# Four layers of memory attention and gated FFN on one core: beta as a row spread by a product, masks of two rounds merged, FFN norms in pairs of tiles, the order planned anew

## The chip, the cores and the metric

One core of one Trainium2 chip. The metric is the device time of one execution in microseconds (us). The time before is the median of three runs. A profile is of one execution; its span runs from the first to the last instruction that the profiler saw, and the execution's own time is a little longer.

## What is computed

`x` is 2048 x 512, bfloat16. Four blocks follow each other, attention, FFN, attention, FFN, each added to `x`, with the same weights both times:

```python
def _A_ref(x, wq, wk, wv, wo, beta):          # on layernorm(x)
    # 32 heads of 16; the sequence is 4 segments of L = 512
    phi = lambda t: jnp.where(t > 0, t + 1.0, jnp.exp(t))
    mask = (ar[:, None] < ar[None, :]) * -1e9
    g = sigmoid(beta)                          # one number for each head
    for s in range(4):
        p = softmax(qs @ ks.T * scale + mask)  # inside the segment
        a_dot = p @ vs
        a_mem = (phi(qs) @ M) / (phi(qs) @ z + 1e-6)
        o = g * a_mem + (1.0 - g) * a_dot
        M, z = M + phi(ks).T @ vs, z + phi(ks).sum()
    return concat(o) @ wo

def _B_ref(x, w_gate, w_up, w_down):           # on layernorm(x), F = 1792
    return (gelu(x @ w_gate) * (x @ w_up)) @ w_down
```

## The kernel before

**Steps.** A segment of 512 rows is four tiles of 128. Each of the 4 segments goes through two layers, so there are 8 attention steps `k` = 0 to 7 (`Att`) and 8 FFN steps (`Ffn`). Attention step k+4 needs FFN step k of the same segment, and step k needs the memory `M`, `z` of step k-1. Attention of later segments and the FFN of earlier ones run interleaved.

**An attention step.** The norm (`Norm`): statistics of the four tiles on VectorE, one small pair of instructions on GpSimd for all four (add eps, power -0.5, L526 and L531), then each tile is scaled (`xn`, L543) and transposed into `xnT`. That last step is either a DMA transpose issued from SP (L436), or four products with the identity on TensorE, `turn_item`, L585, whose result VectorE or ScalarE copies out (L460, L461); `BY_PE` and `pe_turns` say which. In `turn_item`, `FILL` = 2 products of 128 x 256 with the constant tile `warm` stand ahead of a tile's transposes for the steps in `BY_PE` (L583). Then products with w_q, w_k, w_v (L475 as one 128 x 128 product, L470 as four products of 32 columns side by side: function `product` takes the form that saves a change of tiling).

**Scores.** For each group `b` of 8 heads there are `ROUNDS` = 9 rounds of score products (L936): four for the even heads, one shared, four for the odd ones. They run two rounds at a time into four PSUM banks; ScalarE takes the exponential of both (L1394) into slots of `pt`. Rounds that touch the diagonal are masked there: `DIAG` gives 1, 1, 0 or 2 pieces of 64 columns to each of the four (GpSimd, L1341, one instruction for a round), and the shared round is masked whole, by VectorE with a triangle `tri` (L1351) or by GpSimd in two halves (L1346). A `flush` (L952) then multiplies the masked rounds with the values. The extra value columns, which hold `cden` = 1 + exp(beta), give the denominators.

**An FFN step.** w_o products and the addition to `x` (L1025), the norm as above, 14 tiles of w_gate products, whose results are copied to `gel_sb` and later go through gelu, a few of them straight from PSUM (`direct`), 14 tiles of w_up (multiplied in by VectorE, L1090), four tiles of w_down.

**The order.** All instructions are issued by a planner that runs when the kernel is built. `Clocks` and `Engine` keep an estimated time for each engine with a written-out cost for each instruction; `POLICY` holds weights, slacks and due times. TensorE's queue is filled item by item: scores when ScalarE's backlog is small, else the item that is most due and whose inputs are expected to be there, else, while scores remain, a filler product `warm` x `wide`, which computes nothing. The other engines' queues come from posted jobs, the most urgent first. Each queue runs strictly in the order that the planner wrote; waits are semaphores. A DMA transpose is expected to have landed 1.4 us plus `margin` after its issue:

```python
        def told(t2):
            t3 = max(t2 + 1.4 + margin, ck.dma + 1.2)
            ck.at(t3 - 0.2, lambda: landed(t3))
        ck.sp.post(t, slack, (1.45, lambda: nc.sync.dma_start_transpose(out=out(), in_=in_()), told))
```

**The front** is written by hand: the four tiles of segment 0 are loaded by SP and ScalarE's queue, and `beta` behind them from ScalarE's queue, copied to all 128 partitions (`beta_bc`). 15 fillers (L349) run on TensorE meanwhile. ScalarE computes the moments of one tile, then exp(beta) and exp(-beta) (L1200, L1201), then copies out the first two transposed tiles (L598); VectorE copies the other two (L600). The first products with w_k and w_q follow (L907, L912), and from there the planner takes over with starting times for each engine (`ck.pe = 10.45` and so on).

Of the kernel before, what the change touches and what calls it, by code (L numbers as in the profile page):

```python
# [12 lines left out]
ALU = mybir.AluOpType  # L13
# [29 lines left out]
DIAG = [1, 1, 0, 2]  # L43
SHARED = len(FULL)
# [20 lines left out]
FILL = 2  # L65
# [4 lines left out]
    flush_wait=22.067, piece_slack=7.095, kb_slack=20.572, mem_slack=-6.268, margin=2.476, qk_due=0.851,  # L70
    e_q=-1.002, e_k=1.306, exp_slack=-25.092, e_slack=4.951, phi_slack=10.885, gelu_slack=10.893,
    act_evict=5.208, first_evict=-3.627, gate_step=0.016, up_due=0.12, up_step=0.042, down_due=1.978,
    down_step=0.501, upd_due=1.364, kb_act=6.077, vz_slack=-6.198, x_dve=2.604, v0_due=-1.946, x1_at=-38.956,
    x2_at=16.871, x3_at=24.085, x3_load=17.807, direct=4, gelu_tiles=3, look=1.884, lag=0.5, wv_at=4.575,
    xn_pool=3.759, kb_pool=3.166, cut_pool=2.871, at_pool=10.151, pe_turns=2, gate_due=1.051, shun=1.318,
    hold=5, early=5.58, starve=0.305, near=-0.115, cap=2, soon=5.955, columns=1)
# [15 lines left out]
class Engine:  # L92
# [24 lines left out]
    def serve(self, now):  # L117

        self.jobs = [j for j in self.jobs if not j[4]]
        jobs = [j for j in self.jobs if not self.only or j[3] in (None, self.only)]  # L120
        if not jobs:
            return False
        start = max(self.free, min(j[0] for j in jobs) + self.LATENCY)
        if start > now:
            return False
        held = self.rival is not None and self.rival.port > start + 0.25
        job = min((j for j in jobs if j[0] + self.LATENCY <= start + 0.03), key=lambda j: j[0] + j[1] + (
            self.shun if held and isinstance(j[2][0][0], Port) else 0.0))
# [23 lines left out]
        return True  # L152


class Clocks:
# [36 lines left out]
    def serve(self):  # L192

        again = True
        while again:
# [4 lines left out]
            for w in list(self.waiting):  # L200
                if w[0]():
                    self.waiting.remove(w)
                    w[1]()
                    again = True
            first = min(self.engines, key=lambda e: max(e.free, min((j[0] for j in e.jobs), default=1e9)))
            again |= first.serve(self.pe) or any(e.serve(self.pe) for e in self.engines)
# [79 lines left out]
def order(pol, nc, cst, seg, wrk, psp, A_x, A_wq, A_wk, A_wv, A_wo, A_beta, B_x, B_w_gate, B_w_up, B_w_down, out):  # L286
# [15 lines left out]
    beta_bc = cst.tile([P, H], BF16, name="beta_bc")  # L302
# [12 lines left out]
    nc.scalar.dma_start(out=beta_bc[:], in_=A_beta.partition_broadcast(P))  # L315
# [35 lines left out]
    keep_warm(WARM, 0)  # L351

# [41 lines left out]
    def later_constants():  # L394
# [5 lines left out]
        for n, va in enumerate(vaugs[-1:] + vaugs[:-1]):  # L400
            ck.dve.post(12.0 + 3.0 * n, NORMAL, (0.4, lambda va=va: column(va), None))
# [98 lines left out]
    class Norm:  # L500
        def __init__(self, key, tt0, tag, slack, free):
            self.key, self.tt0, self.tag, self.slack, self.free = key, tt0, tag, slack, free
            self.mv, self.n, self.left = None, 0, TPS
# [4 lines left out]
        def stats(self, j, ready):  # L508
# [14 lines left out]
        def scales(self, ready):  # L523
            def first():
                self.ve = wrk.tile([P, TPS, 1], F32, tag="lnve", name="ve")
                nc.gpsimd.tensor_scalar(out=self.ve[:], in0=self.mv[:, :, 1:2], scalar1=EPS_LN, scalar2=None,  # L526
                                        op0=ALU.add)

            def second():
                self.rs = self.small("rs", 1)  # L530
                nc.gpsimd.tensor_tensor(out=self.rs[:], in0=self.ve[:], in1=mhalf[:], op=ALU.pow)  # L531

            ck.pool.post(ready, URGENT, (0.25, first, None),
                         (1.05, second, lambda t: ck.when(self.free, lambda: self.start(max(t, ck.pe)))))

        def start(self, ready):
            self.xnT = seg.tile([P, KT, L], BF16, tag=self.tag, bufs=1, name="xnT")
            for j in range(TPS):
# [35 lines left out]
        def turn_item(self, j, xn, t, landed):  # L574
# [7 lines left out]
            fill = FILL if self.key in BY_PE else 0  # L582
# [26 lines left out]
    class Att:  # L609
# [14 lines left out]
        def add_items(self):  # L624
# [54 lines left out]
            def v(j):  # L679
# [23 lines left out]
                def vz_sent(t):  # L703
                    self.n_vz += 1
                    t2 = max(t + 1.4 + pol.margin, ck.dma + 1.2)
                    if self.n_vz == 2:
# [3 lines left out]
                            lambda: ck.has(("xnTa", k, j)) and (k or ck.pe > max(pol.wv_at, 12.4)) and (k <= SETS or ("flush", k - SETS, 3, 1) in ev),  # L710
# [229 lines left out]
        def flush_item(self, b, par, places, masked):  # L940
# [4 lines left out]
            def mm():  # L945
                ck.tiling("columns")
                work = [(i + par * (SHARED + 1), self.vaug, *piece) for i, pieces in enumerate(FULL) for piece in pieces]
# [252 lines left out]
    nc.scalar.activation(out=tmp_e, in_=beta_bc[:], func=ACT.Exp)  # L1200
    nc.scalar.activation(out=tmp_e2[:], in_=beta_bc[:], func=ACT.Exp, scale=-1.0)  # L1201

# [18 lines left out]
    n0.first_turn(1)  # L1221
    n0.first_turn(2)
# [16 lines left out]
    ck.pe, ck.act.free, ck.dve.free, ck.pool.free, ck.sp.free = 10.45, 10.75, 10.5, 8.1, 7.6  # L1239
    banks[0:4] = [10.8, 9.45, 9.9, 10.4]  # L1240
    ev["q", 0, 0] = 10.35
    a0.n_qkv = 2
    a0.k_done(0, None, 10.75)
    later_constants()
    ck.dma = 13.0
# [18 lines left out]
    norm_of_input(1, max(pol.x1_at, 10.4), 0.5)  # L1264
    norm_of_input(2, max(pol.x2_at, 13.2), 1.0)
# [73 lines left out]
    def mask(slot, n):  # L1339
        view = pt_all[:, slot, :, 0:C * n].rearrange("p u (t c) -> p u t c", c=C)  # L1340
        nc.gpsimd.affine_select(out=view, in_=view, pattern=[[0, 4], [0, n], [1, C]], compare_op=ALU.is_ge,  # L1341
# [7 lines left out]
    def mask_both(slot):  # L1349
        view = pt_all[:, slot, :, :].rearrange("p u (t c) -> p (u t) c", c=C)  # L1350
        nc.vector.tensor_tensor(out=view, in0=view, in1=tri[:].unsqueeze(1).to_broadcast([P, 4 * TPS, C]), op=ALU.mult)  # L1351

    def post_mask(slot, t, at, done):
        n = round_of(t)[3]
        if n is None:
            taken = []
            ck.dve.post(at, pol.x_dve, (Port(0.67), lambda: mask_both(slot), done.append), taken=taken)
            ck.pool.post(at, NORMAL, (Port(1.14), lambda: mask_half(slot, 0), None), (Port(1.14), lambda: mask_half(slot, 1), done.append),
                         taken=taken)
        elif n:  # L1360
            ck.pool.post(at, NORMAL, (Port(0.245 + 0.215 * n), lambda: mask(slot, n), done.append))
        else:
            done.append(at)

    def score(n):
# [22 lines left out]
        for p, pair in enumerate(pairs):  # L1388
            score_banks.update(pair)
            for i in pair:  # L1390
                banks[i] = 1e9

            def exp(p=p, pair=pair):
                nc.scalar.activation(  # L1394
                    out=pt_all[:, s0:s0 + 2, 2 * p:2 * p + 2, :].rearrange("p r h c -> p h r c"),
# [127 lines left out]
```

## Time and profile before

| | |
|---|---|
| median of three runs | 549.18 us (548.96 to 549.21) |
| the profiled execution | 549.09 us, its span 547.4 us |
| TensorE products / weight loads | 533.9 / 277.9 us busy |
| VectorE, ScalarE, GpSimd | 444.8, 435.9, 307.4 us busy |
| DMA | 27.02 MB, 49 GB/s on average; 88 of the issues are transposes |

PE is TensorE, PEld its weight loads, DVE VectorE, ACT ScalarE, POOL GpSimd, SP the queue that issues most DMAs. A row of a group gives line, engine, operation, result and operands, shape, count, then busy time and mean length in ns of one, then the idle time of that engine before them with what ended it. Products are pipelined: one that is followed by another takes the time from its start to the next start, which is shorter than its own length.

### The profile page before, as it was taken

The page shows a single profiled execution, that of the slowest core. Times are in us where ns is not written, and L with a number is a line of the kernel's source. Part 1 is how long each engine was busy: PE and PEld are TensorE (multiplying, and loading weights), DVE is VectorE, ACT ScalarE, POOL GpSimd, SP SyncE. Part 2 cuts the span into 40 slices and gives each one's busy share as a digit, 9 for nine tenths or more (in the row PEclk, how much of TensorE's full clock was granted, in tenths as well). Part 3 has the DMA queues.
Part 4 walks back from the last instruction along what each step waited for, and adds up shares of the span by engine and source line. Part 5 has one row for each costly group of instructions (what it writes and reads, how often), then busy time and mean ns, then how long its engine had stood idle before and what let it go on. Part 6 is the DMA issues. An engine that isn't in the chain of part 4 may idle for free.

```text
span 547.4 us, 22326 instructions
## 1 busy us (share of the span) xinstructions
PE 533.9 (98%) x9794; PEld 277.9 (51%) x9852; DVE 444.8 (81%) x823; ACT 435.9 (80%) x545; POOL 307.4 (56%) x359
## 2 busy tenths in 40 slices
PE   8999999999999999999999999999999999999997
PEld 4454555454544455444544555544464455555544
DVE  6999898899999899759997887988888786686342
ACT  5899989988899987989899898897889984830330
POOL 2789489579843766528882487927874043400000
PEclk9999999999999999999999999999999999999999
DMA  8407600711231113501222241211311005100001
GB/s 254 111 2 178 151 12 3 175 42 23 50 50 22 23 32 51 79 2 25 41 31 40 32 61 23 31 38 36 70 48 28 2 10 89 26 4 21 20 0 40
DMA packets 64930, 27.02 MB, mean 49 GB/s; under 512 B 49216, under 2 KB 64832, under 8 KB 64832
## 3 DMA queue, kind: packets, MB, share of 16 engines
q1 hardware_dynamic: 64400, 25.31, 22.7%
q8 instruction: 77, 1.26, 1.0%
q10 hardware_dynamic: 432, 0.27, 0.2%
q14 instruction: 21, 0.17, 0.1%
HBM read 9.71 MB, written 2.10 MB: 22 GB/s over the span
## 4 chain that ended last, share of the span: by engine, by line
PE 85%; DVE 9%; issue 2%; DMA 2%; ACT 2%; POOL 0%; SPq 0%; DVEq 0%; POOLq 0%; ACTq 0%
PE ps L475 41%; PE ps L470 30%; PE ps L936 7%; PE ps L952 6%; DMA x_sb<-in_A_x_dram 2%; DVE st L513 2%; ACT pt L1394 1%; DVE x_sb L1025 1%; DVE byq L969 1%; DVE xn L543 1%; PE ps L585 1%; DVE phiq L743 1%; PE ps L583 1%; DVE vaug L460 0%; DVE kf L460 0%
## 5 line engine op out<-in xcount | busy, mean ns | idle before, releaser
L1394 ACT ACTIVATE pt<-ps 128x1024 bf16<-128x1024 f32 x288 | 279.7, 1028 | 41.0 <-PE ps L936 32.3
L1341 POOL TENSOR_SCALAR_AFFINE_SELECT pt<-pt 128x256 bf16<-128x256 bf16 (+1 forms) x192 | 111.9, 597 | 128.5 <-ACT pt L1394 126.8
L1090 DVE TENSOR_TENSOR gel_sb<-gel_sb,ps 128x512 bf16<-128x512 bf16 x112 | 74.5, 682 | 27.0 <-PE ps L475 21.3
L1346 POOL TENSOR_SCALAR_AFFINE_SELECT pt<-pt 64x1024 bf16<-64x1024 bf16 x50 | 60.9, 1218 | 11.8 <-ACT pt L1394 7.8
L475 PE MATMUL ps<-xnT,wg_sb 128*128 128x512 bf16 x266 | 63.6, 380 | 1.2 <-issue 0.8
L475 PE MATMUL ps<-xnT,wu_sb 128*128 128x512 bf16 x265 | 62.2, 380 | 1.5 <-issue 1.1
L1025 DVE TENSOR_TENSOR x_sb<-x_sb,ps 128x512 bf16<-128x512 bf16 (+1 forms) x68 | 43.0, 644 | 23.7 <-PE ps L475 16.7
L969 DVE STREAM_TRANSPOSE byq<-ps 128x512 f32<-128x512 f32 x64 | 45.3, 709 | 20.9 <-PE ps L952 18.9
L470 PE MATMUL ps<-wd_sb,gel_sb 128*32 128x512 bf16 (+1 forms) x1012 | 54.6, 356 | 0.0
L475 PE MATMUL ps<-wd_sb,gel_sb 128*128 128x512 bf16 (+1 forms) x240 | 49.8, 355 | 1.6 <-issue 1.6
L762 POOL TENSOR_SCALAR e<-e 128x512 bf16<-128x512 bf16 x29 | 46.0, 1587 | 1.1
L475 PEld LDWEIGHTS <-wu_sb 128*128 128x128 bf16 x278 | 25.9, 98 | 31.2 <-issue 1.1
L470 PE MATMUL ps<-xnT,wg_sb 128*32 128x512 bf16 x676 | 41.2, 380 | 0.0
L513 DVE BATCH_NORM_STATS2 st<-x_sb 128x6 f32<-128x512 bf16 x60 | 40.3, 672 | 1.0 <-DMA x_sb<-in_A_x_dram 0.9
L475 PEld LDWEIGHTS <-wg_sb 128*128 128x128 bf16 x279 | 25.8, 98 | 29.7 <-issue 0.6
L470 PE MATMUL ps<-xnT,wu_sb 128*32 128x512 bf16 x680 | 38.6, 379 | 0.0
L416 POOL TENSOR_SCALAR kx<-kf,masks 128x512 bf16<-128x512 bf16 x22 | 35.0, 1592 | 2.0 <-ACT kf L461 0.8
L952 PE MATMUL ps<-pt,vaug 128*32 128x256 bf16 (+2 forms) x1344 | 35.0, 238 | 0.0
L470 PEld LDWEIGHTS <-gel_sb 128*32 128x32 bf16 x1012 | 25.3, 97 | 17.7 <-issue 1.3
L475 PEld LDWEIGHTS <-gel_sb 128*128 128x128 bf16 x251 | 23.3, 98 | 21.6 <-issue 0.4
L1149 ACT ACTIVATE gel_sb<-gel_sb 128x1536 bf16<-128x1536 bf16 (+1 forms) x28 | 33.5, 1283 | 0.0
L543 DVE TENSOR_SCALAR xn<-x_sb,mv,rs 128x512 bf16<-128x512 bf16 x57 | 28.0, 538 | 6.3 <-POOL rs L531 4.0
(148 smaller groups left out, 899.0 us busy)
## 6 DMA issues: line engine op xcount, KB each, us to landing
vz<-vaug SPq DMA_DIRECT2D x14, 136.0 KB, 2.6
wg_sb<-in_B_w_gate_dram SPq DMA_DIRECT2D x8, 224.0 KB, 3.8
wu_sb<-in_B_w_up_dram SPq DMA_DIRECT2D x8, 224.0 KB, 3.8
wd_sb<-in_B_w_down_dram SPq DMA_DIRECT2D x7, 256.0 KB, 4.1
x_sb<-in_A_x_dram SPq DMA_DIRECT2D x3, 512.0 KB, 7.4
out_dram<-x_sb SPq DMA_DIRECT2D x12, 128.0 KB, 1.7
xnT<-xn SPq DMA_TRANSPOSE x40, 2.7
wk_sb<-in_A_wk_dram SPq DMA_DIRECT2D x2, 256.0 KB, 6.0
```

The costliest lines, as they stand in the source:

```text
L470: nc.tensor.matmul(out[r], lhsT=lhsT[:, r], rhs=rhs, start=start, stop=stop, tile_position=(0, 32 * c))
L475: nc.tensor.matmul(out, lhsT=lhsT, rhs=rhs, start=start, stop=stop)
L513: nc.vector.bn_stats(out=self.st6[:, 0, :], in_=x_sb[:, self.tt0 + j, :])
L762: lambda eng: eng.tensor_scalar(out=e[0][:], in0=e[0][:], scalar1=1.0, scalar2=None, op0=ALU.min), summed)
L936: nc.tensor.matmul(ps_all[:, bank, o + c0:o + c0 + n], lhsT=lhsT, rhs=self.q[rows, b, q0:q0 + n], start=True, stop=True, tile_position=(32 ...
L952: nc.tensor.matmul(ps()[32 * j:32 * j + 32, q0:q0 + n], lhsT=va[:, ki * VW + g:ki * VW + g + 32], rhs=pt_all[:, places[i], j, c0:c0 + n], ...
L969: nc.vector.transpose(out=self.byq[:, par, :, :].rearrange("p a c -> p (a c)"), in_=ps()[:])
L1025: ck.dve.post(ck.made(), slack, (0.15 + 0.00104 * (c1 - c0), lambda: nc.vector.tensor_tensor(out=xt, in0=xt, in1=ps()[:, 0:c1 - c0], op=AL ...
L1090: ck.dve.post(ck.made(), NORMAL, (0.683, lambda: nc.vector.tensor_tensor(out=g, in0=g, in1=ps()[:], op=ALU.mult), lambda t: (ps.read(t), e ...
L1341: nc.gpsimd.affine_select(out=view, in_=view, pattern=[[0, 4], [0, n], [1, C]], compare_op=ALU.is_ge, fill=0.0, base=C, channel_multiplier=-1)
L1346: nc.gpsimd.affine_select(out=view, in_=view, pattern=[[0, 4 * TPS], [1, C]], compare_op=ALU.is_ge, fill=0.0, base=0, channel_multiplier=-1)
L1394: nc.scalar.activation(out=pt_all[:, s0:s0 + 2, 2 * p:2 * p + 2, :].rearrange("p r h c -> p h r c"), in_=ps_all[:, pair[0]:pair[1] + 1, :] ...
```

## The change

The change has five parts; all but the first and the starting times act through the planner, so that nearly every queue's order differs.

1. `beta` is loaded as one row of one partition; a product of a row of ones with it on TensorE, ahead of the first transposes, spreads it over 128 partitions into a PSUM bank. The two exponentials read it from there and stand behind ScalarE's copies of the first two transposed tiles.
2. The rounds of scores are permuted (`ORDER`) so that two rounds which run together often have the same number of masked pieces; such two are masked by one GpSimd instruction. The shared round is masked on GpSimd by one product with `tri` in place of two halves.
3. The norm of an FFN step adds eps and takes the power for two tiles at a time, and starts to scale and transpose these two; an attention step's norm stays at four. `FILL` is 0.
4. The planner's costs and times are changed: 1.3 for 1.45 us for a DMA transpose, other starting times at the front, the jobs that write `cden` into the value tiles 9.985 us apart with w_v's products waiting for them, the most overdue engine served first.
5. `POLICY` has new values, among them `pe_turns` 0 for 2 (the attention steps 1 and 2 are transposed by DMA), `margin` 2.253, `direct` 3, `gelu_tiles` 4.

```diff
+ORDER = [[(0, 1, 2, 3), (2, 0, 1, 3)], [(3, 0, 1, 2), (0, 1, 2, 3)]]
...
-    return b, (par,), FULL[i - par * (SHARED + 1)], DIAG[i - par * (SHARED + 1)]
+    n = ORDER[b % 2][par][i - par * (SHARED + 1)]
+    return b, (par,), FULL[n], DIAG[n]
...
-    nc.scalar.dma_start(out=beta_bc[:], in_=A_beta.partition_broadcast(P))
+    nc.scalar.dma_start(out=beta_row[:], in_=A_beta.partition_broadcast(1))
...
     keep_warm(WARM, 0)
+    beta_ps = ps_all[:, BANKS - 1, 0:H]
+    nc.tensor.matmul(beta_ps, lhsT=warm[0:1, :], rhs=beta_row[:], start=True, stop=True)
...
-            ck.dve.post(12.0 + 3.0 * n, NORMAL, (0.4, lambda va=va: column(va), None))
+            ck.dve.post(10.0 + pol.col_gap * n, URGENT if n < 1 else NORMAL,
+                        (Port(0.5), lambda va=va: column(va), lambda t, n=n: ev.update({("column", n): t})))
...
-        ck.sp.post(t, slack, (1.45, lambda: nc.sync.dma_start_transpose(out=out(), in_=in_()), told))
+        ck.sp.post(t, slack, (1.3, lambda: nc.sync.dma_start_transpose(out=out(), in_=in_()), told))
...
+            self.group = 2 if key[0] == "xnTf" else TPS
...
             def told(t):
-                self.n += 1
-                if self.n == TPS:
-                    self.scales(t)
+                g = j // self.group
+                self.n[g] += 1
+                if self.n[g] == self.group:
+                    self.scales(t, slice(g * self.group, (g + 1) * self.group))
...
-            fill = FILL if self.key in BY_PE else 0
+            fill = pol.fill if self.key in BY_PE and self.key[1] < NK - 1 else 0
...
-    nc.scalar.activation(out=tmp_e, in_=beta_bc[:], func=ACT.Exp)
-    nc.scalar.activation(out=tmp_e2[:], in_=beta_bc[:], func=ACT.Exp, scale=-1.0)
...
     n0.first_turn(0)
     n0.first_turn(1)
+    nc.scalar.activation(out=tmp_e, in_=beta_ps, func=ACT.Exp)
+    nc.scalar.activation(out=tmp_e2[:], in_=beta_ps, func=ACT.Exp, scale=-1.0)
     n0.first_turn(2)
...
-    ck.pe, ck.act.free, ck.dve.free, ck.pool.free, ck.sp.free = 10.45, 10.75, 10.5, 8.1, 7.6
+    ck.pe, ck.act.free, ck.dve.free, ck.pool.free, ck.sp.free = 10.1, 10.6, 10.5, 8.1, 6.5
...
+    def mask(slot, n, rounds):
+        view = pt_all[:, slot:slot + rounds, :, :].rearrange("p s u c -> p (s u) c")[:, :, 0:C * n].rearrange(
+            "p u (t c) -> p u t c", c=C)
+        nc.gpsimd.affine_select(out=view, in_=view, pattern=[[0, 4 * rounds], [0, n], [1, C]], compare_op=ALU.is_ge,
                                 fill=0.0, base=C, channel_multiplier=-1)
...
+    def post_masks(marks, at):
+        n = [round_of(t)[3] for _, t, _ in marks]
+        if len(marks) == 2 and n[0] and n[0] == n[1]:
+            ...
+            ck.pool.post(at, NORMAL, (Port(0.245 + 0.43 * n[0]), lambda: mask(marks[0][0], n[0], 2), both))
+            return
+        for (slot, _, done), n in zip(marks, n):
+            if n is None:
+                taken = []
+                ck.dve.post(at, pol.x_dve, (Port(0.67), lambda slot=slot: mask_both(slot), done.append), taken=taken)
+                if pol.x_whole:
+                    ck.pool.post(at, NORMAL, (Port(2.3, True), lambda slot=slot: mask_both(slot, nc.gpsimd), done.append),
+                                 taken=taken)
```

What the two programs issue, counted in their instruction orders:

| | before | after |
|---|---|---|
| TensorE: full-width fillers after the front / half-width fillers | 33 / 24 | 42 / 0 |
| TensorE: transposes after the front | 80 | 48 |
| TensorE: changes of tiling | 301 | 298 |
| SP: DMA transposes | 88 | 96 |
| GpSimd: masks of rounds (single, merged) | 192, 0 | 32, 80 |
| shared rounds masked by VectorE / GpSimd halves / GpSimd whole | 7 / 50 / 0 | 13 / 0 / 19 |
| GpSimd: powers of the norms after the front | 15 | 23 |
| copies out of PSUM and xnT copies on ScalarE (L461) / VectorE (L460) | 88 / 96 | 77 / 106 |
| ScalarE: gelus of steps 0 to 6 (from `gel_sb`, from PSUM) | 28, 28 | 21, 21 |

More of the change, by code (lines that the diff above doesn't have):

```diff
@@ L199, in serve @@
                 again = True
[L200 to L206, printed above, removed]
+            if self.waiting:
+                for w in list(self.waiting):
+                    if w[0]():
+                        self.waiting.remove(w)
+                        w[1]()
+                        again = True
+            best = None
+            for e in self.engines:
+                if e.jobs:
+                    t = e.next_start()
+                    if t is not None and t <= self.pe and (best is None or t < best):
+                        best, first = t, e
+            if best is not None:
+                first.serve(best)
+            elif not again:
+                return
     def dma_load(self, t, kb):
@@ L301, in order @@
     gel_sb = cst.tile([P, FT, L], BF16, name="gel_sb")
-    beta_bc = cst.tile([P, H], BF16, name="beta_bc")
+    beta_row = cst.tile([1, H], BF16, name="beta_row")
     def load(dst, src):
@@ L502, in __init__ @@
             self.key, self.tt0, self.tag, self.slack, self.free = key, tt0, tag, slack, free
[L503 removed]
+            self.mv, self.rs, self.xnT, self.left = None, None, None, TPS
+            self.group = 2 if key[0] == "xnTf" else TPS
+            self.n = [0] * (TPS // self.group)
         def small(self, name, width):
@@ L709, in v @@
                 return Item(lambda: k - pol.qk_due + 0.04 + 0.01 * j if k else pol.v0_due,
-                            lambda: ck.has(("xnTa", k, j)) and (k or ck.pe > max(pol.wv_at, 12.4)) and (k <= SETS or ("flush", k - SETS, 3, 1) in ev),
+                            lambda: ck.has(("xnTa", k, j)) and (k or ck.pe > max(pol.wv_at, 11.5)) and
+                            ck.has(("column", min(k, SETS)), by=ck.pe + 0.9) and (k <= SETS or ("flush", k - SETS, 3, 1) in ev),
                             dense(ps, pairs), done, kind="v", ps=ps, after=("xnTa", k, j))
```

146 lines of the change are left out of this document (79 added, 67 removed).

## The prediction

> **What bounds the kernel now.** I read the page's busy times first, then busy time by stretches of the span, then TensorE's waits, then its instructions in order of time.
>
> ```profile
> span 547.4 us, 22326 instructions
> ...
> PE 533.9 (98%) x9794; PEld 277.9 (51%) x9852; DVE 444.8 (81%) x823; ACT 435.9 (80%) x545; POOL 307.4 (56%) x359
> ```
>
> ```profile
> core 0: us, PE busy (x) PEld busy (x) DVE busy (x) ACT busy (x) POOL busy (x), PEclk, DMA share, GB/s
> 0.00:10.50 10.50, 8.80 (x48) 4.34 (x49) 6.75 (x22) 5.04 (x12) 3.64 (x15) 1.00 0.76 224
> 10.50:50.00 39.50, 37.79 (x580) 18.82 (x592) 36.25 (x83) 37.80 (x53) 31.36 (x36) 1.00 0.37 94
> 50.00:478.00 428.00, 421.23 (x8503) 220.23 (x8545) 367.13 (x660) 377.82 (x461) 269.92 (x306) 1.00 0.24 46
> 478.00:544.00 66.00, 65.79 (x676) 34.52 (x671) 34.21 (x59) 15.22 (x23) 2.44 (x3) 1.00 0.05 16
> 544.00:547.40 3.40, 0.24 (x3) 0.00 (x0) 0.42 (x1) 0.00 (x0) 0.00 (x0) 1.00 0.13 39
> ```
>
> TensorE is idle 1.71 us between 10.5 and 50, 6.77 between 50 and 478 and 0.21 from there to its last matmul: 8.7 us of open waiting in 533.5. No other engine comes near that. So the time is TensorE's own instructions one behind the other, and an edit is worth what it takes out of that row, at the front, or out of the 8.7 us.
>
> ```profile
> PE ps L475 <- issue: 4.9, 31, 0.2
> PE ps L349 <- DVE warm L340: 1.1, 1, 1.1
> PE ps L936 <- ACT pt L1394: 0.7, 1, 0.7
> PE ps L475 <- DVE byq L969: 0.7, 1, 0.7
> ```
>
> Most of the 8.7 us is "issue", 31 pieces of at most 0.2 us where the array changes its tiling; waits for another engine are single and under 1 us. But TensorE's row also holds products that compute nothing: fillers, put where the planner saw nothing ready. There the waiting is planned, and the profile calls it busy. That is what the change can shorten.
>
> **Prices on TensorE**, from its instructions in order of time (start, duration, line, count):
>
> ```profile
> 471.71 1.47 PE L475 MATMUL ps<-xnT,wg_sb 128*128 128x512 bf16 x6
> 473.11 0.40 PE L936 MATMUL ps<-q,kx 32*128 32x256 bf16 x12
> ...
> 478.24 12.26 PE L470 MATMUL ps<-xnT,wu_sb 128*32 128x512 bf16 x224
> 490.33 3.63 PE L470 MATMUL ps<-wo_sb,aT 128*32 128x512 bf16 x64
> 493.78 6.22 PE L470 MATMUL ps<-wd_sb,gel_sb 128*32 128x512 bf16 x112
> 499.93 0.39 PE L583 MATMUL ps<-warm 128*128 128x256 bf16 x2
> 500.16 0.39 PE L585 MATMUL ps<-ident,xn 128*128 128x128 bf16 x4
> 500.38 0.38 PE L583 MATMUL ps<-warm 128*128 128x256 bf16 x2
> ```
>
> From start to start: 224 column matmuls are 56 products in 12.09 us, 0.216 each; a whole-array product costs as much, so which of the two forms a product takes is free. Two half-width fillers take 0.23 us, 0.115 each; four transposes 0.22 us, 0.055 each. Six whole products from 471.71 to 473.11 take 1.40 us, 0.105 more than 6 x 0.216: that is one change of tiling. The groups by shape bound the small ones from above, since they count the last one's full pipeline:
>
> ```profile
> L585 PE MATMUL ps<-ident,xn 128*128 128x128 bf16 x80 | 7.1, 220 | 0.2 <-ACT pt L1394 0.2
> L583 PE MATMUL ps<-warm 128*128 128x256 bf16 x24 | 4.8, 275 | 0.0
> ```
>
> That is at most 0.089 and 0.20. I take the spacings, as these stand in a packed row.
>
> **Fillers and transposes, place by place.** Every real product is the same in both programs; the instruction order of the two differs in these counts. Inputs of segments 1 and 2 (about 18 to 30 us): 4 full fillers and 32 transposes before, 9 fillers and no transpose after; 4 x 0.216 + 32 x 0.055 = 2.62 becomes 1.94, -0.68. First FFN norm (about 74 to 83 us): 20 full and 8 half fillers become 22 full: 5.24 to 4.75, -0.49. Second FFN norm: 9 full and 8 half become 11 full: 2.86 to 2.37, -0.49. Last norm (500 us): 8 half become none, -0.92. The 48 transposes of the FFN norms stay. Sum -2.58; with the upper prices -4.1. Changes of tiling go from 301 to 298, the two around the beta product among them: -0.3.
>
> What covers the wait once the fillers are gone: at the last norm, the first pair of tiles now goes through its norm under the 12.26 us of w_up products, and the second pair's chain stands under 28 w_down products, 6.0 us by 0.216. What that chain takes, from VectorE's first addition after w_o to its last scaled tile, the kernel before shows for four tiles:
>
> ```profile
> 491.42 0.69 DVE L1025 TENSOR_TENSOR x_sb<-x_sb,ps 128x512 bf16<-128x512 bf16 x1 [0.18 <-PE ps L470]
> 498.71 1.38 DVE L543 TENSOR_SCALAR xn<-x_sb,mv,rs 128x512 bf16<-128x512 bf16 x4 [0.92 <-POOL rs L531]
> ```
>
> 500.09 - 491.42 = 8.67 us for four, so some 4.3 to 5 for two: covered. At the two earlier norms there is no such cover; there the shorter chain must itself come true.
>
> **The front.** ScalarE's and VectorE's rows at the start:
>
> ```profile
> 6.55 0.72 PE L595 MATMUL ps<-ident,xn 128*128 128x128 bf16 x8
> 7.05 0.23 ACT L1200 ACTIVATE macc<-beta_bc 128x32 f32<-128x32 bf16 x1 [1.25 <-DMA beta_bc<-in_A_beta_dram]
> 7.30 1.06 ACT L598 ACTIVATE xnT<-ps 128x512 bf16<-128x512 bf16 x2
> 8.00 0.76 DVE L600 COPY xnT<-ps 128x512 bf16<-128x512 bf16 x2 [0.17 <-PE ps L595]
> 8.42 0.60 PE L907 MATMUL ps<-xnT,wk_sb 128*128 128x256 bf16 x4
> 9.05 0.38 ACT L1226 ACTIVATE wd_sb<-ps 128x256 bf16<-128x256 f32 x1 [0.69 <-PE ps L907]
> ```
>
> ScalarE stands 1.25 us on beta's load and the two exponentials keep its copies of the first two transposed tiles back to 7.30. The first four transposes are done at 6.55 + 3 x 0.055 + the last one's own 0.22 = 6.94. With the exponentials behind the copies these start there, 0.35 us sooner, and L907 with them; the exponentials fall into ScalarE's 0.69 us hole before L1226. VectorE's copies (8.76) are needed only by the fifth group of products, so nothing takes the 0.35 back. On TensorE the new beta product stands ahead of the transposes: behind it is all of TensorE if beta comes late. Beta's 128 small pieces landed 5.3 us after their issue (row below), at 7.05; one row can hardly be later. So -0.35 to +0.2 (transposes from 7.1 on instead of 6.55); I take -0.35, since one short piece issued at 1.7 should land nearer the 2.7 us of the first inputs.
>
> **Transposes moved to SP.** Eight more DMA transposes, for segments 1 and 2; the load of the fourth input segment now goes out between the two groups, and loads of w_o and w_gate between those of the second.
>
> ```profile
> x_sb<-in_A_x_dram SPq DMA_DIRECT2D x3, 512.0 KB, 7.4
> xnT<-xn SPq DMA_TRANSPOSE x40, 2.7
> beta_bc<-in_A_beta_dram ACTq DMA_DIRECT2D x1, 8.0 KB, 5.3
> ...
> DMA to landing us min/median/max: 2.4/2.7/4.5
> ```
>
> The kernel's 40 transposes of such tiles landed 2.4 to 4.5 us after issue, and the planner of the changed kernel counts on 1.3 + 1.4 + 2.253 = 4.95. So by these rows none is late: 0. The other end is a tile that lands like the 512 KB input loads, at 7.4, which is 2.45 us late for a segment, 4.9 for both. I take 0: 4.5 is the worst of 40. The Trainium skill, "DMA: Bandwidth & Descriptors", section "Queues, rings and completion order", says that on each DMA engine the descriptors of one issuing queue are consumed in ring order; a transpose issued behind a load on SP then waits for that load. By that rule the second group behind the 512 KB load is the one at risk; no transpose of this trace stands directly behind so large a load.
>
> **Masks, norms, evictions.** GpSimd's groups:
>
> ```profile
> L1341 POOL TENSOR_SCALAR_AFFINE_SELECT pt<-pt 128x256 bf16<-128x256 bf16 x128 | 64.4, 516 | 71.7 <-ACT pt L1394 70.3
> L1341 POOL TENSOR_SCALAR_AFFINE_SELECT pt<-pt 128x512 bf16<-128x512 bf16 x64 | 48.5, 758 | 56.8 <-ACT pt L1394 56.5 <-DVE zcols L880 0.3
> L1346 POOL TENSOR_SCALAR_AFFINE_SELECT pt<-pt 64x1024 bf16<-64x1024 bf16 x50 | 60.9, 1218 | 11.8 <-ACT pt L1394 7.8 <-PE ps L475 2.4
> L531 POOL TENSOR_TENSOR rs<-ve,mhalf 128x4 f32<-128x4 f32 x15 | 15.7, 1047 | 1.3
> L987 POOL TENSOR_TENSOR aT<-aT,amT 128x512 bf16<-128x512 bf16 x12 | 14.2, 1186 | 17.5 <-DVE aT L984 17.3
> L1191 POOL TENSOR_TENSOR rs<-mv,mhalf 128x2 f32<-128x2 f32 x2 | 1.5, 752 | 2.5 <-DVE mv L1187 2.5
> ```
>
> Masks cost 173.8 us now. After: 64 merged of 512 elements (0.758), 32 single ones (0.758), 16 merged of 1024 (about 1.22) and 19 products with the triangle, each twice L987, 2.37: 48.5 + 24.3 + 19.5 + 45.0 = 137. GpSimd is freed of 37 us, and it waited for ScalarE before most masks: nothing on TensorE, 0. A merged mask gives its first round 0.24 us later and its second 0.27 sooner. The norm in pairs costs 0.75 instead of 1.05 us for the power and one more pair of small instructions; its worth is already in the filler counts. ScalarE loses 11 evictions, VectorE gets 10 (0.68 each, 6.8 us of the 103 us that it has idle), 0. If that cover were gone, each would put its 0.68 us into a TensorE wait for a bank.
>
> **Sum.** 549.09 of the profiled execution (median of the runs 549.18, so no correction) - 2.58 - 0.3 - 0.35 = 545.9, with the 8.7 us of open waits as they are. Two of this order's waits may be shorter and two longer; that I can't see.
>
> **Rivals.** (1) The fillers only stood for waits: at the three early places TensorE now stands still as long as it was filled. Against it: each place has other fillers in the new order. Then only the last norm's 0.92, the 0.3 and the 0.35 are left: 547.5. (2) The new order waits more in the body, as its planner judged by changed costs: 8.7 us grow by 30%, 2.6 us: 548.5. For it: all of the order is new; against it: waits for engines are now few and short. (3) Slower: transposes behind loads, 18 to 35 us. Both segments' tiles land at 7.4 as the ring rule would have it: 545.9 + 4.9 = 550.8; it decides when the two are together over 4.3 us late, and one segment alone gives 548.4. Against it: 4.5 us at worst in 40 transposes, some issued between w_gate and w_up loads.
>
> **Chances.** The runs spread by 0.05%; about 0.2%, 1.1 us, can be told from no change, so faster means under 548.0. Forecast 0.62, nearly all faster; rival 1 0.15, two thirds faster; rival 2 0.13, mostly the same; rival 3 0.10, mostly slower. Faster 0.74, same 0.15, slower 0.11. Low end: the forecast with 2.5 us of the open waits gone, 543.4; high end 549.4, above rival 2, leaves out most of rival 3.
>
> **What would show it.** Right: TensorE busy near 531 us; L907 at about 8.05; idle between 10.5 and 544 still 8 to 10 us; the last norm without a gap. Wrong: a TensorE wait for a DMA of xnT at 18 to 35 us (rival 3); waits at 70 to 83 or 127 to 135 us ahead of the transposes (rival 1); TensorE idle of 11 us and more spread over the body (rival 2); transposes at the front later than 6.6 us (beta).

## The result, and the profile after

The changed kernel takes 554.36 us (median of six runs, 553.06 to 554.94) against 548.89 for the kernel before (six runs, 548.59 to 549.21): a ratio of 1.0096, 95% interval 1.0083 to 1.0109. It is slower by 5.5 us where 545.9 was forecast: outside the range, and on the other side. The profiled execution took 554.50 us, its span 552.8.

The page's span, busy times and TensorE's granted clock in 40 slices:

```profile
span 552.8 us, 22911 instructions
PE 532.0 (96%) x10128; PEld 282.3 (51%) x10181; DVE 463.1 (84%) x831; ACT 431.6 (78%) x522; POOL 287.7 (52%) x270
PEclk9999999999989999999999999999999999999999
```

TensorE is busy 1.9 us less than before and the span is 5.4 us longer (552.8 against 547.4): the time is, in the main, not in its instructions but between them. VectorE is busy 18.3 us more, though only 8 instructions were added, and one slice of 14 us shows a clock below full. Busy time by the prediction's stretches:

```profile
0.00:10.50 10.50, 8.28 (x60) 4.46 (x60) 6.95 (x24) 5.21 (x12) 3.63 (x15) 1.00 0.85 255
10.50:50.00 39.50, 37.82 (x714) 18.85 (x710) 37.05 (x78) 37.18 (x51) 32.63 (x28) 1.00 0.55 123
50.00:478.00 428.00, 414.51 (x8671) 222.30 (x8714) 381.04 (x667) 369.31 (x435) 248.87 (x223) 1.00 0.23 45
478.00:544.00 66.00, 65.79 (x669) 33.01 (x666) 36.18 (x63) 19.88 (x27) 2.54 (x5) 1.00 0.07 14
```

Idle time of TensorE is the length less the first figure: 1.68 (before 1.71), **13.49 (6.77)** and 0.21 (0.21). The whole loss lies in the body. The next view is the same kind of table for the body alone, cut at the places where the change took fillers out (18 to 35, 68 to 90, 122 to 145 us). First the kernel before, then the changed one:

```profile
18.00:35.00 17.00, 16.35 (x270) 8.72 (x274) 15.36 (x40) 17.00 (x26) 14.96 (x17) 1.00 0.29 77
68.00:90.00 22.00, 21.95 (x516) 12.46 (x516) 19.77 (x38) 20.46 (x27) 19.60 (x21) 1.00 0.04 9
122.00:145.00 23.00, 22.44 (x401) 11.51 (x401) 22.53 (x44) 19.63 (x28) 20.34 (x22) 1.00 0.09 18
145.00:478.00 333.00, 328.13 (x6717) 171.12 (x6754) 279.12 (x501) 291.74 (x352) 197.53 (x230) 1.00 0.23 38
```

```profile
18.00:35.00 17.00, 16.84 (x405) 8.80 (x399) 15.43 (x33) 16.35 (x24) 13.88 (x12) 1.00 0.51 97
68.00:90.00 22.00, 21.66 (x518) 12.06 (x517) 21.45 (x40) 20.66 (x26) 18.89 (x18) 1.00 0.14 29
122.00:145.00 23.00, 20.04 (x415) 11.02 (x417) 22.34 (x39) 18.64 (x24) 18.96 (x17) 1.00 0.08 16
145.00:478.00 333.00, 323.85 (x6845) 173.94 (x6874) 292.04 (x510) 283.25 (x331) 183.20 (x165) 0.99 0.21 38
```

Idle before 0.65, 0.05, 0.56 and 4.87; after 0.16, 0.34, **2.96** and **9.15**. TensorE's longest waits in the changed kernel:

```profile
PE ps L502 <- issue: 4.4, 28, 0.2
PE ps L971 <- DVE x_sb L1061: 2.2, 2, 1.6
PE ps L619 <- DVE xn L577: 2.1, 1, 2.1
...
PE ps L971 <- DVE gel_sb L487: 0.9, 2, 0.8
PE ps L497 <- ACT pt L1444: 0.9, 1, 0.9
PE ps L497 <- DVE kf L487: 0.7, 1, 0.7
PE ps L971 <- DVE gel_sb L1126: 0.7, 1, 0.7
PE ps L988 <- DVE macc L928: 0.6, 1, 0.6
PE ps L497 <- DVE phiq L778: 0.5, 1, 0.5
```

The "issue" line is the old one (4.9 before); the dots stand for two lines of the front. Of the new lines of half a microsecond and more, all but one of 0.9 us for ScalarE, which stays in the versions without the loss, name VectorE; GpSimd is in none. So the list names whom TensorE waited for, and not why that engine was late. Its instructions in order of time around the 2.1 us wait say why (GpSimd, VectorE and TensorE, start and duration):

```profile
137.73 2.13 POOL L1387 TENSOR_TENSOR pt<-pt,tri 128x1024 bf16<-128x1024 bf16 x1
137.90 2.51 DVE L1013 TENSOR_TENSOR ab<-byq,r 128x512 bf16<-128x512 f32 x1
140.33 1.22 DVE L911 TENSOR_TENSOR mblk<-macc,bd 128x512 bf16<-128x512 f32 x1
141.48 0.76 DVE L577 TENSOR_SCALAR xn<-x_sb,mv,rs 128x512 bf16<-128x512 bf16 x1
142.29 0.40 PE L619 MATMUL ps<-ident,xn 128*128 128x128 bf16 x4 [2.13 <-DVE xn L577]
147.95 0.69 DVE L1013 TENSOR_TENSOR ab<-byq,r 128x512 bf16<-128x512 f32 x1
```

The same VectorE operation, `ab`, takes 0.69 us at 147.95 and 2.51 at 137.90, where it starts 0.17 us after GpSimd's shared-round product. That product ends at 139.86, and `ab` at 140.41, 0.55 us behind it, a little less than its own 0.69. So VectorE did not work for 2.5 us: by these times it stood still until GpSimd was through. Everything behind `ab` in its queue came 1.8 us late, among it the third `xn` tile, which TensorE's transposes need.

This is no single case. Between 10.5 and 478 us TensorE waits eight times for 0.5 us or more on VectorE, 7.5 us together. Each of the eight stands 2 to 5 us behind a VectorE operation (two of them behind the same one) that ran beside a shared-round product of GpSimd and took 1.75 to 2.60 us, where its kind takes 0.35 to 0.69 at the median.

### The profile page after: what moved, and what is told of

Read it like the earlier page. It is cut to its first block, busy times and chain, and to the rows that moved or that the text cites. A ratio compares the mean times of both kernels' runs of the same rounds, so it can differ in the third digit from the quotient of the medians.

```text
span 552.8 us, 22911 instructions
## 1 busy us (share of the span) xinstructions
PE 532.0 (96%) x10128; PEld 282.3 (51%) x10181; DVE 463.1 (84%) x831; ACT 431.6 (78%) x522; POOL 287.7 (52%) x270
## 4 chain that ended last, share of the span: by engine, by line
PE 63%; DVE 7%; issue 3%; POOL 1%; ACT 0%; DVEq 0%; ACTq 0%
PE ps L502 27%; PE ps L497 27%; PE ps L971 5%; PE ps L988 4%; DVE x_sb L1061 1%; DVE ab L1013 1%; DVE st L542 1%; DVE gel_sb L1126 1%; DVE byq L1005 1%; DVE phiq L778 0%; DVE e L778 0%; DVE gel_sb L487 0%; DVE aT L1020 0%; ACT pt L1444 0%; PE ps L619 0%
## 5 line engine op out<-in xcount | busy, mean ns | idle before, releaser
L1377 POOL TENSOR_SCALAR_AFFINE_SELECT pt<-pt 128x512 bf16<-128x512 bf16 (+1 forms) x112 | 95.6, 857 | 95.6 <-ACT pt L1444 94.1
L502 PE MATMUL ps<-wd_sb,gel_sb 128*128 128x512 bf16 (+1 forms) x318 | 68.7, 360 | 1.3 <-issue 0.6
L797 POOL TENSOR_SCALAR e<-e 128x512 bf16<-128x512 bf16 x37 | 58.8, 1590 | 4.4 <-ACT e L774 3.5
L497 PE MATMUL ps<-xnT,wg_sb 128*32 128x512 bf16 x852 | 52.6, 389 | 0.0
L1387 POOL TENSOR_TENSOR pt<-pt,tri 128x1024 bf16<-128x1024 bf16 x19 | 41.3, 2174 | 16.1 <-ACT pt L1444 16.1
L1023 POOL TENSOR_TENSOR aT<-aT,amT 128x512 bf16<-128x512 bf16 x15 | 17.3, 1159 | 45.5 <-DVE aT L1020 19.9
L487 DVE CAST gel_sb<-ps 128x512 bf16<-128x512 f32 x57 | 37.5, 679 | 3.8 <-PE ps L497 2.9
L1185 ACT ACTIVATE gel_sb<-gel_sb 128x2048 bf16<-128x2048 bf16 (+1 forms) x21 | 36.1, 1776 | 0.0
L497 PE MATMUL ps<-wd_sb,gel_sb 128*32 128x512 bf16 (+1 forms) x684 | 35.3, 346 | 0.0
L971 PEld LDWEIGHTS <-kx 32*128 32x128 bf16 x1120 | 17.8, 92 | 31.3 <-issue 30.7
```

What stands on the lines that cost most here:

```text
L497: nc.tensor.matmul(out[r], lhsT=lhsT[:, r], rhs=rhs, start=start, stop=stop, tile_position=(0, 32 * c))
L502: nc.tensor.matmul(out, lhsT=lhsT, rhs=rhs, start=start, stop=stop)
L797: lambda eng: eng.tensor_scalar(out=e[0][:], in0=e[0][:], scalar1=1.0, scalar2=None, op0=ALU.min), summed)
L971: nc.tensor.matmul(ps_all[:, bank, o + c0:o + c0 + n], lhsT=lhsT, rhs=self.q[rows, b, q0:q0 + n], start=True, stop=True, tile_position=(32 ...
L1377: nc.gpsimd.affine_select(out=view, in_=view, pattern=[[0, 4 * rounds], [0, n], [1, C]], compare_op=ALU.is_ge, fill=0.0, base=C, channel_m ...
L1387: eng.tensor_tensor(out=view, in0=view, in1=tri[:].unsqueeze(1).to_broadcast([P, 4 * TPS, C]), op=ALU.mult)
```

## The experiments

**1. What does the shared round's product cost in this order?** Every queue is kept as planned; in each of the 19 places GpSimd gets the two halves of the kernel before.

```diff
-                    ck.pool.post(at, NORMAL, (Port(2.3, True), lambda slot=slot: mask_both(slot, nc.gpsimd), done.append),
+                    ck.pool.post(at, NORMAL, (Port(2.3, True), lambda slot=slot: (mask_half(slot, 0), mask_half(slot, 1)), done.append),
```

> The changed kernel, each queue's order unchanged; the 19 shared rounds that GpSimd masks are masked by two affine selects in place of one product with the triangle. Theory A (GpSimd's product shuts VectorE out of a shared resource for its whole 2.2 us; in the changed kernel's trace VectorE's instructions that run beside it are 1.7 us longer): VectorE's busy time falls from 463 to some 450 us, TensorE's idle time between 10.5 us and its last matmul shrinks from 17 to about 10 us, no stretch of half clock at 157 to 161 us, time 548 to 550. Theory B (the new order waits more because all its times are a little off and VectorE has more to do): VectorE's holds get shorter but TensorE's waits stay; time within 1.5 us of 554.4.

Measured 547.89 us against 549.02: 0.9979 [0.9970, 0.9989]. The sign of the change turns on this one instruction: 6.5 us lower than the changed kernel. VectorE's busy time fell less than expected, to 459.0 us, and TensorE's idle time in the body from 13.49 to 8.99:

```profile
50.00:478.00 428.00, 419.01 (x8823) 225.25 (x8866) 383.21 (x677) 373.14 (x439) 253.01 (x241) 1.00 0.24 45
```

**2. The same product in the old order.** The kernel before, with GpSimd's two halves replaced by one product.

```diff
-    def mask_both(slot):
+    def mask_both(slot, eng=nc.vector):
...
-            ck.pool.post(at, NORMAL, (Port(1.14), lambda: mask_half(slot, 0), None), (Port(1.14), lambda: mask_half(slot, 1), done.append),
+            ck.pool.post(at, NORMAL, (Port(1.14), lambda: mask_both(slot, nc.gpsimd), None), (Port(1.14), lambda: None, done.append),
```

> The kernel before, each queue's order unchanged; the 25 shared rounds that GpSimd masks (50 halves) are masked by one product with the triangle each. Theory A: VectorE is held up by about 1 us in most of 25 places, its busy time rises by some 15 us, and TensorE waits more: 551 to 555. Theory B: GpSimd takes the same 2.2 to 2.4 us for either form, so 549, as before.

Measured 549.11 against 549.02: 1.0002 [0.9991, 1.0012], and the expectation of a loss failed. VectorE is held here too: its busy time is

```profile
PE 533.9 (97%) x9794; PEld 277.5 (51%) x9852; DVE 453.2 (83%) x823; ACT 436.0 (79%) x545; POOL 303.4 (55%) x334
```

453.2 instead of 444.8 us. But TensorE does not wait on it: although this profiled execution was the longest of the ten (551.02 us), its list of waits has no line on VectorE that the kernel before lacks. A held VectorE cost time only where the order has its result due at once; the new order has such places (the eight above), the old one did not.

**3. The front alone.** The kernel before with part 1 of the change (beta's row and product, the exponentials moved).

> The kernel before with part 1 alone: beta as a row spread by a product, the exponentials behind the first two copies; the planned order is untouched. If the front's gain stays: the first products with w_k start at 8.2 in place of 8.42, and 548.6 to 548.8 against 548.9. If it is lost again at the load of w_v (TensorE waits for it at 12.9 already): 548.9. Neither moves by more than 0.4 us.

Measured 548.07 against 549.02: 0.9981 [0.9970, 0.9991], a gain of 0.95 us and more than expected. In the profiled execution (548.56 us) the first products are not earlier (the first `wk_sb` products at 8.47 us instead of 8.42); the gain is in the next 10 us, here before and with the new front:

```profile
10.50:20.00 9.50, 8.30 (x75) 3.81 (x78) 8.33 (x23) 7.93 (x13) 4.89 (x6) 1.00 0.43 141
```

```profile
10.50:20.00 9.50, 8.86 (x78) 4.14 (x81) 9.10 (x27) 8.70 (x13) 4.89 (x6) 1.00 0.36 117
```

TensorE is idle 0.64 us there instead of 1.20. Loads of the weights and inputs land sooner (`wk_sb` after 5.2 us instead of 6.0, `x_sb` after 6.9 instead of 7.4). It is no chance of one execution: in the profiles of this order with beta on 128 partitions `wk_sb` takes 6.0 to 6.6 us (experiments 2 and 8 too), with the row 5.2 and 5.3 (experiment 9). That 128 pieces of beta no longer stand among the loads fits, but was not shown.

**4. Planned with halves.** The changed kernel with `x_whole=0`: the planner lays out a new order around two halves.

> The changed kernel with x_whole = 0: the planner knows that GpSimd masks a shared round in two halves of 1.14 us, and works out the order anew with all other values as they are. Theory A: no product on GpSimd, so waits near 9 us: 546 to 549.5. Theory B: the new costs and values make a poor order whatever the mask: 551 to 556.

Measured 555.76 against 549.02: 1.0120 [1.0105, 1.0135]. This is the second expectation, a poor order whatever the mask, and it says nothing of the halves. The planner put in 92 fillers after the front in place of 42, 50 x 0.216 = 10.8 us, and TensorE's busy time rose to 539.8 us:

```profile
PE 539.8 (98%) x10266; PEld 285.9 (52%) x10324; DVE 453.8 (82%) x824; ACT 432.5 (78%) x526; POOL 291.4 (53%) x289
```

So the parts can't be priced by planning anew; all other experiments keep an order fixed and change what is issued in it.

**5 and 10. Is it the product, or its length?** The changed order with the same product cut into two pieces of 512 columns, then into four of 256 (the edit for four).

```diff
+    def mask_cols(slot, u):
+        view = pt_all[:, slot, u:u + 1, :].rearrange("p u (t c) -> p (u t) c", c=C)
+        nc.gpsimd.tensor_tensor(out=view, in0=view, in1=tri[:].unsqueeze(1).to_broadcast([P, TPS, C]), op=ALU.mult)
...
-                    ck.pool.post(at, NORMAL, (Port(2.3, True), lambda slot=slot: mask_both(slot, nc.gpsimd), done.append),
+                    ck.pool.post(at, NORMAL, (Port(2.3, True), lambda slot=slot: [mask_cols(slot, u) for u in range(4)], done.append),
```

> The changed kernel, queues unchanged, but each GpSimd product with the triangle is cut into two products of 512 columns each. Theory A1 (VectorE is shut out until the one GpSimd instruction ends, and gets in between two): holds of at most some 1.1 us, time 548 to 550, near the run with two affine selects (547.9). Theory A2 (it is the kind of instruction, one with two operands in SBUF, that shuts VectorE out, and the second half follows at once): 553 to 555, as the changed kernel.

> The changed kernel, queues unchanged, each GpSimd product with the triangle cut into four of 256 columns. Theory A1 (VectorE is held until the one instruction ends) has 1 piece 554.4, 2 pieces 549.1, so 4 pieces 547.5 to 548.6. If only the sum of GpSimd's time counts: four fixed costs more, 549.5 to 551.

Two pieces: 549.07 against 549.21, 1.0003 [0.9993, 1.0012]. Four pieces: 546.75 against 549.17, 0.9957 [0.9942, 0.9972], the lowest median of all, below both kernels and below the range expected. One piece 554.4, two 549.1, four 546.7: same values, same engine, same queues. What costs is how long one GpSimd instruction lasts. GpSimd's own work even grows, from 41.3 to 56.7 us (the changed kernel, then four pieces):

```profile
L1387 POOL TENSOR_TENSOR pt<-pt,tri 128x1024 bf16<-128x1024 bf16 x19 | 41.3, 2174 | 16.1 <-ACT pt L1444 16.1
```

```profile
L1391 POOL TENSOR_TENSOR pt<-pt,tri 128x256 bf16<-128x256 bf16 x76 | 56.7, 775 | 9.3 <-ACT pt L1448 9.3
```

The same place in order of time, with four pieces:

```profile
136.97 0.69 DVE L1013 TENSOR_TENSOR ab<-byq,r 128x512 bf16<-128x512 f32 x1
138.67 0.76 DVE L577 TENSOR_SCALAR xn<-x_sb,mv,rs 128x512 bf16<-128x512 bf16 x1
```

Here `ab` starts 0.43 us ahead of the first piece (137.40), so this place alone does not show what a short piece does. `phiq`, also with two inputs in SBUF, does: both times it starts 0.29 us behind the start of GpSimd's work on a shared round. First the changed kernel, then four pieces:

```profile
151.97 2.13 POOL L1387 TENSOR_TENSOR pt<-pt,tri 128x1024 bf16<-128x1024 bf16 x1
152.26 2.39 DVE L778 SCALAR_TENSOR_TENSOR phiq<-q,e 128x512 bf16<-128x512 bf16 x1
```

```profile
149.81 3.45 POOL L1391 TENSOR_TENSOR pt<-pt,tri 128x256 bf16<-128x256 bf16 x4
150.10 0.93 DVE L778 SCALAR_TENSOR_TENSOR phiq<-q,e 128x512 bf16<-128x512 bf16 x1
```

2.39 us become 0.93, VectorE gets in between two pieces, and TensorE's wait for this `phiq` is gone. The body's stretches with four pieces:

```profile
18.00:35.00 17.00, 16.84 (x399) 8.78 (x401) 15.47 (x33) 16.35 (x23) 14.47 (x15) 1.00 0.56 97
68.00:90.00 22.00, 21.78 (x518) 12.10 (x518) 20.41 (x40) 20.55 (x27) 20.10 (x24) 1.00 0.20 33
122.00:145.00 23.00, 22.32 (x500) 12.41 (x495) 22.53 (x43) 20.62 (x27) 22.00 (x25) 1.00 0.10 18
145.00:478.00 333.00, 327.44 (x6941) 176.23 (x6976) 291.04 (x517) 286.02 (x332) 187.66 (x203) 1.00 0.23 39
```

TensorE is idle 0.16, 0.22, 0.68 and 5.56 us: within 0.7 us of the kernel before in each stretch, with 2.28 and 3.59 us of the changed kernel's waits gone from the last two.

**6. The merged masks undone as well.** Experiment 1, with each merged mask issued as two single ones.

> As the run with two affine selects in the new order, and each merged mask of two rounds issued as two single masks at the same place. If merging is worth something on TensorE's path: slower by 0.5 to 2 us (about 548.5 to 550), GpSimd busy about 20 us more. If the masks are hidden as predicted, or the shorter instruction lets VectorE in sooner: 547 to 548, the same.

Measured 548.52 against 549.21: 0.9990 [0.9980, 1.0000], where experiment 1 had 0.9979. By medians merging is worth about half a microsecond, but the intervals overlap. It is not where the time went.

**7 and 8. What do the fillers stand for?** Both leave out only the fillers after the front, which compute nothing: the 42 of the new order (with the halves of experiment 1), and the 33 full and 24 half ones of the old.

> As the run with two affine selects in the new order, with the 42 fillers after the front left out (9.1 us of products that compute nothing); all other queues unchanged. If the fillers stand for waits that are there (the first rival of the prediction): TensorE's idle time grows by what they took, 547.5 to 548.5. If the planner puts more fillers than waits: down to 541 to 545.

> The kernel before with its 33 full and 24 half fillers left out (9.9 us by 0.216 and 0.115). If they stand for waits: 548.5 to 549.5. If not: 541 to 546. The difference to the same edit of the new order tells whether the new order's saving in fillers (prediction: 0.92 at the last norm, 0.49 at each of the two first FFN norms) was a saving in time.

550.22 against 549.21, 1.0018 [1.0006, 1.0029], and 550.33, 1.0024 [1.0014, 1.0034]. Both are slower than the same order with its fillers: by 2.3 us against experiment 1, by 1.1 against the kernel before, by medians, and above what either expectation allowed for waits. The granted clock of the two profiles:

```profile
PEclk9999979999799999999999999999999999999999
```

```profile
PEclk9999988999999999999999999999999999999999
```

Where the fillers were, TensorE now waits (2.7 us at the longest, for `xn` in the second FFN norm of the new order), and the clock is down: in the new order in the slices of both early FFN norms, in the old one in those of the first. The fillers that are left do not cost what they take; they hold a place that would be a wait, and the clock with it.

**9. The front and the last norm.** Experiment 3, and the 8 half fillers of the last norm left out.

> The kernel before with part 1 (beta as a row) and without the 8 half fillers ahead of the last norm's transposes; everything else as before. The prediction put 0.92 us on those fillers, because four tiles are scaled by then and w_down products follow. If that holds: 547.1 against 548.07 of part 1 alone, faster than before by 0.3%. If they too stand for a wait: 548.1.

Measured 547.38 against 549.17: 0.9967 [0.9955, 0.9979], 0.7 us under experiment 3, by medians; the two intervals overlap. Both parts together give 1.8 us; the forecast for them was 0.35 + 0.92 = 1.27.

## Why the prediction was wrong

**The step that failed: "nothing on TensorE, 0" for the masks.** It priced the shared round's product in GpSimd's time (2.37 us by twice L987; it took 2.17) and asked only whether GpSimd had room. That price held: the masks took 95.6 + 41.3 = 136.9 us, and 137 were forecast. But the cost falls on VectorE, and through it on TensorE: `ab` rose from 0.69 to 2.51 us beside one product, and each form of it was measured beside its own runs of the kernel before: whole 5.47 us above them, in two pieces 0.14 below (no difference by its interval), as halves 1.13 below, in four pieces 2.42 below. The forecast missed by 8.5 us; the whole product, against four pieces, is 7.9 of them.

The Trainium skill bears on this, "SBUF — State Buffer", section "SBUF: two separate sides": VectorE and GpSimd share one pair of ports, an exclusive lock: where a VectorE operation with two inputs in SBUF meets a GpSimd one that reads SBUF, the first to start has it for the whole instruction, and the other engine stands still. The rows agree: `ab`, started 0.17 us into the 2.13 us product, ended 0.55 us after it. I had not weighed that page, though the change lengthens exactly such an instruction, from halves of 1.22 us to 2.17.

**The cover was counted over the wrong stretch.** "The 103 us that it has idle" is VectorE's idle time over the whole span. From 122 to 145 us, where 2.4 of the 6.7 us are lost, the prediction's own kind of table shows next to none: VectorE is busy 22.53 of 23.00 us, before the change already, and the holds went into a full queue. The other 4.3 us are lost between 145 and 478 us, where VectorE has more idle time (busy 279.12 of 333 us before, 292.04 after); idle time elsewhere does not bring sooner the one result that TensorE waits for. How much of either the ten more evictions cost is not shown. Experiment 2 shows the other side: the same product in the old order, with VectorE's busy time up by 8.4 us, costs nothing measurable.

**A second cost came with the waits, in some executions.** After the waits at 142.29, 154.71 and 156.38 us the profiled execution ran part of the next group at half clock:

```profile
158.00:160.00 2.00, 2.00 (x24) 0.83 (x20) 1.38 (x4) 1.98 (x3) 1.13 (x1) 0.50 0.00 0
```

This group is the same in the run with four pieces (TensorE in order of time, the changed kernel, then four pieces):

```profile
156.69 5.97 PE L497 MATMUL ps<-xnT,wg_sb 128*32 128x512 bf16 x76
```

```profile
153.08 4.28 PE L497 MATMUL ps<-xnT,wg_sb 128*32 128x512 bf16 x76
```

That is 1.69 us, and the profile calls it busy. From 10.5 to 478 us TensorE is idle 15.17 us here and 8.76 with four pieces, 6.41 more; with the 1.69, and less the 0.78 us by which the front was later in the execution with four pieces, that makes 7.3 of the 7.7 us between the two spans (552.8 and 545.1). The half clock is not in every execution of the changed kernel: the three with a mean clock of 0.996 or 0.997 took 554.50 to 554.94 us, the three with 1.0 took 553.06 to 554.21. The waits alone thus make most of the loss.

**The step for fillers, transposes and tilings held.** With four pieces, TensorE is busy 531.4 us ("near 531"), and nothing opened at the three early places: idle there was 0.65 + 0.05 + 0.56 = 1.26 before, and is 1.06. (The other figure of that step, -4.1 "with the upper prices", is a slip: 33 x 0.216 + 24 x 0.20 + 32 x 0.089 less 42 x 0.216 is 5.7. The forecast did not use it.) Rival 1 (waits where the fillers were) is false for the fillers that the change takes out, since there the shorter chain is real; it is true for those that remain, by experiments 7 and 8. In the changed kernel itself there is a wait ahead of the transposes at 142.29, but the held VectorE made it.

**The last norm held:** idle from 478 to 544 us stayed 0.21, and experiment 9 gained 0.7 us by medians where 0.92 was forecast; by the intervals of experiments 3 and 9 it can't be told more closely.

**The front was right in sign, and in part by luck.** In the changed kernel's profile beta was not late, ScalarE's copies began at 7.07 instead of 7.30 us, and L942 (L907 before) at 8.21 instead of 8.42, where 8.05 was forecast:

```profile
5.79 0.18 PE L377 MATMUL ps<-beta_row,warm 1*128 1x32 bf16 x1
6.63 0.72 PE L629 MATMUL ps<-ident,xn 128*128 128x128 bf16 x8 [0.66 <-DVE xn L577]
8.21 0.60 PE L942 MATMUL ps<-xnT,wk_sb 128*128 128x256 bf16 x4
```

L942's start differs from one execution to the next: 8.23 in experiment 9, 8.47 in experiment 3, 8.98 in experiment 10. The transposes started at 6.63, 6.66, 6.90 and 7.41 us in these four profiles, later than 6.6 as the prediction's sign of a late beta has it, but beta held none of them. In the first two they waited for `xn`; in the other two the 15 fillers ahead of them ended late, at 6.9 and 7.4 us (5.9 in the changed kernel's profile), as more of them took 0.63 us in place of 0.38. So the 0.95 us of experiment 3 is not the 0.35 that was forecast: its first products are no earlier. The late start also fits what experiment 10 lacks of the forecast: its first scores began at 11.06 us instead of 10.49, and 549.09 - 2.58 - 0.3 + 0.57 = 546.8, where that execution took 546.86.

**Rival 2** (waits of 11 us and more in the body) came true in its number, 15.2 us from 10.5 to 478, and not in its reason: kept with another form of one instruction, the same order waits 8.8 us. **Rival 3** is false: 48 DMA transposes landed in 2.7 us at the median and 4.2 at the worst (40 before, 2.7 and 4.5), no wait of TensorE names one, and the stretch of 18 to 35 us is the one that became better. A transpose right behind the 512 KB load was not put to the test: the first one after it was issued 5.7 us later (30.98 and 25.28 us).

```profile
xnT<-xn SPq DMA_TRANSPOSE x48, 2.7
```

What brought the product in is seen in the diff: the planner books it as `Port(2.3, True)`, a soft claim on the port by which VectorE loses 0.15 us in the plan, where the halves were hard claims of 1.14. The chip took up to 1.91 (`phiq`, 2.60 us for 0.69, at 410.82 us). Still open: what the other parts (permuted rounds, new weights) are worth one by one, since every new plan moves all queues; and why the front alone gains 0.95 us, of which its profile shows 0.5.

## What to carry to other kernels

Price an instruction of an engine that is off the path also by whom it holds while it runs: on GpSimd the length of one instruction counted here, not their sum, and cutting the same work into four turned 5.5 us of loss into 2.4 of gain. Take the cover for a cost from the stretch where it falls; an engine 81% busy over the span was 98% busy in the 23 us where a third of the loss fell. Filler products that a planner has placed are waits with a name: see first whether the chain behind them became shorter, then count them as saved.

## What the runs showed of the hardware

- A VectorE operation with two inputs in SBUF, started beside a GpSimd product of 2.13 us, lasted until that product ended and 0.55 us more: `ab` 2.51 and `phiq` 2.39 us, both 0.69 at the median. In the kernel before, whose masks last 0.5 to 1.2 us at the mean, the worst of the 32 `ab` took 0.90 us (the worst `phiq` 1.64, beside a half of 1.14):

```profile
L977 DVE TENSOR_TENSOR ab<-byq,r x32: 691/692/903, 33.0 to 479.6; 128x512 bf16<-128x512 f32 x32
```

- Cut into pieces, GpSimd's product costs more in sum (19 of 2.174 us whole, 76 of 0.775 us in four, which is 41.3 against 56.7 us in the groups above) and less for the kernel.
- TensorE's clock fell after shorter waits than I had thought: in the changed kernel the longest single wait near it is 2.13 us, with 3.47 us idle of the 20 from 140 to 160 us and a mean clock of 0.94 there:

```profile
140.00:160.00 20.00, 16.53 (x357) 8.62 (x358) 18.96 (x31) 15.42 (x20) 14.95 (x12) 0.94 0.18 35
```

The Trainium skill, "TensorE: Matmul & The Clock Gate", Part 1, puts the fall behind an idle window of about 3.4 us, and also tells of a kernel in which frequent short idle times between groups of products made the clock go up and down. No single wait here was 3.4 us long; several stood close together, and in half of the executions the mean clock stayed at 1.0 all the same. With four pieces, where these waits are gone, it was 0.999 or 1.0 in all five. Which of the waits brings the fall is not shown.
